# Attention's stores and weight loads on SyncE's queue: when they are issued, and at which heads the side work stands

## The chip, the cores and the metric

The kernel runs on one core of a Trainium2 chip. The metric is the device time of one execution in microseconds (us). The kernel before was run three times: 2304.03, 2305.62 and 2310.8 us, median 2305.62. One further execution was profiled.

The engines go by the profile's names: PE is TensorE's matrix unit, PEld its weight loads, DVE is VectorE, ACT is ScalarE, POOL is GpSimd and SP is SyncE, which here issues every DMA. Each engine runs its own instructions in one fixed order and waits in place for whatever the next one needs. SP does so too, so a DMA whose source is not ready holds up every DMA that stands behind it in SP's order.

## The reference, cut to what matters

```python
h = layernorm(x) * (1 + ca) + sa              # sa, ca, ga, sb, cb, gb = rows of silu(c) @ w_mod
x = x + ga * attention(h)                     # 32 heads of 32, 4 segments of 512 tokens, with a memory
h = layernorm(x) * (1 + cb) + sb
x = x + gb * mixer_mlp(h)                     # an MLP over the 2048 tokens, F = 3584

def attention(h):                             # per head, for s in 0..3:
    p = softmax(q_s @ k_s.T * scale + mask)   # strictly upper triangle masked
    o_s = g * (phi(q_s) @ M / (phi(q_s) @ z + 1e-6)) + (1 - g) * (p @ v_s)
    M, z = M + phi(k_s).T @ v_s, z + sum(phi(k_s))
    return concat(o) @ wo
```

x is 2048 x 1024 in float32. Products are made from operands split into a high and a low part (`split`, L116), three matmuls for one.

## The kernel before, in words

There are three stages: attention, the output projection (`out_proj`, L688), and two large products of the MLP (`mix`, L783). The change touches the first alone.

**How attention is cut.** Four heads of the model make a group `g` (8 groups). A segment of one group is a unit of work `t`; `its` (L313) lists 32 of them: pass 0 takes each group through segments 0 and 1, pass 1 takes each through segments 2 and 3. Head number n = 4t + h runs from 0 to 127. The main loop (L621) goes over n from -3 to 128 and writes down, for each n, the scores of head n, the row maxima of head n + 3, the values of head n - 1 and one of four pieces of projection of the unit that is eight heads ahead.

- `project(t, piece)` (L329): pieces 0 and 1 are the k/v products (`nps`, `kv_chunk` L186, 48 matmuls of 256 columns each; one half takes weight parts v0 for the first 24 and v1 for the others), piece 2 transposes k (`kps`, L363), makes the q product (`qps`, L201, 24 matmuls of 512 columns), splits both into `sg` and calls `stack` for three heads; piece 3 stacks the fourth head and updates the memory. The bank of a k/v product comes free when DVE has subtracted from it (`r`, L356).
- `stack(t, h)` (L319): three DMAs `sk<-sg` (L325 to L327) that lay one head's q and k out for its scores.
- `maxima(t, h)` (L421): products `sx`, `sy`, `sz`, maxima on DVE (L432), and after every second head a transpose `nmps`, two small tiles `nt` (ACT L440, DVE L441) and four DMAs `sk<-nt` (L445), without which the scores of the two heads can't start.
- `scores(t, h)` (L459): products `a` (L466 to L473), exponentials `p` on ACT, the triangle on POOL (L477), a split into `ph` (ACT L479, POOL L481).
- `values(t, h)` (L483): products `pv`; after the fourth head `ot` is copied by ACT (L512) and stored to DRAM (L513).

**Side work at listed heads.** `plan(n, f, engines)` (L594) puts f at head n; `later` (L597) plans a fetch at one head and its use at another. `behind` (L451) lets what f issues on the engines named stand behind the instruction that `marks` keeps for that head: A, G and V stand for ACT, POOL and DVE. The list holds: eight token tiles of the segments of pass 1 (`token_tile`, L227, in the one buffer `gaw`, one tile every 5 heads, stored at once by L246); weights of groups 2 to 7 for pass 0, fetched, split and stored for pass 1 in one go (`keep_w`, L171); 32 tiles of late rows of w_mod (`mod_late`, L523) at heads 40, 42, ... 102; eight pieces of wo (`wo_fetch`, `wo_split`, L575 and L581) at heads 65, 71, ... 107. These share three buffers named `raw`.

**Weights of the second pass.** `load_w` (L176) is called from the loop four heads before a group's first piece stands in it: all six tiles of the group (`wv<-wsp`, `wq<-wsp`, L168) are written down at once. There are eight buffers, so that the last four tiles wait until the group before has been used.

**What sets the order.** The program's order is a priority. A scheduler with a time model walks all engines and gives each the first instruction in that order that its model has ready, so work is pulled ahead where an engine would stand idle. `tc.issue_after(i)` adds the demand that what follows stands behind i on i's engine. What comes out is fixed before the program runs. Where the model's times and the chip's differ, the engine waits.

Of the kernel before, what the change touches and what calls it, by code (L numbers as in the profile page):

```python
# [31 lines left out]
VL = 1  # L32
PHB = 2
P32B = 2
ML0 = 40
MLS = 2
HB = 3
WO0 = 65
WOS = 6
WCT = 5  # L40
LEADP = 8
LEADS = 3
# [2 lines left out]
def attention_and_mlp(ctx, tc, x, wq, wkv, wo, beta, w1, b1, w2, b2, c, wm_a, wm_b, out):  # L45
# [112 lines left out]
            split(w, r[:, 512 * i:512 * i + 512], A, V)  # L158
            W[0, g][kind, 2 * part + i] = w

    def load_part(g, pr, kind, part, res):

        if pr == 0:
            split_part(g, kind, part, fetch_part(g, kind, part))
            return
        for i in range(2):
            w = aw.tile([P, 2, 512], F32R, tag="w", bufs=8, name=f"w{kind}{pr}_{g}_{part}_{i}")
            SY.dma_start(w.bitcast(F32), wsp[g, 2 * part + i if kind == "v" else 4 + i])  # L168
            res[kind, 2 * part + i] = w

    def keep_w(g):  # L171
        for kind, n in (("v", 4), ("q", 2)):
            for i in range(n):
                SY.dma_start(wsp[g, i if kind == "v" else 4 + i], W[0, g][kind, i].bitcast(F32))

    def load_w(g, pr):  # L176
        res = W[pr, g] = {}
        for kind, part in (("v", 0), ("v", 1), ("q", 0)):
            load_part(g, pr, kind, part, res)
        if pr == 0:  # L180
            keep_w(g)

    W = {}

# [42 lines left out]
    def token_tile(tt):  # L227

        r = gaw
        norm_x(a, r)  # L230
        for half in range(2):
            ps = bank("s2", 2, f"hpl{tt}_{half}")
            for i in range(4):
                ct = 4 * half + i
                T.transpose(ps[:, 128 * i:128 * i + 128], r[:, P * ct:P * ct + P], ident)
            for i in range(4):
                ct = 4 * half + i
                A.activation(r[:, P * ct:P * ct + P], ps[:, 128 * i:128 * i + 128], AF.Identity,
                             scale=saca[:, ct, 1:2], bias=saca[:, ct, 0:1])
        hi = a.tile([P, D], F32, tag="raw", bufs=3, name=f"hix{tt}")  # L240
        A.copy(hi.bitcast(F32R), r)
        for c in (slice(0, 512), slice(512, 1024)):
            G.tensor_tensor(r[:, c].bitcast(F32R), r[:, c], hi[:, c], op=ALU.subtract)
        i = tt % 4
        for part, t in enumerate((hi, r)):
# [28 lines left out]
    for ct in range(NK):  # L274
        for part in range(2):
            wm = s1p.tile([P, D], F32, tag="wm", bufs=11, name=f"wm{ct}_{part}")
            last_wm = SY.dma_start(wm, wm_a[part, ct])
            if part == 0:
                V.scalar_tensor_tensor(wm, wm, 1.0, scb, op0=ALU.mult, op1=ALU.mult, accum_out=saca[:, ct, 0:1])
            else:  # L280
                for k in range(NK):
                    T.matmul(scale_ps[:, ct:ct + 1], wm[:, P * k:P * k + P], sc[:, k:k + 1], start=(k == 0),
                             stop=(k == NK - 1), skip_group_check=True)
        if ct < 3:
            load_part(0, 0, *(("v", 0), ("q", 0), ("v", 1))[ct], W[0, 0])
# [29 lines left out]
    st = {}  # L315

    last_sk = {}

    def stack(t, h):  # L319
# [7 lines left out]
        last_sk[t, h] = SY.dma_start(skf[64:96], src[:, 1:3])  # L327

    def project(t, piece):  # L329
        pr, g, seg = its[t]  # L330
# [90 lines left out]
    def maxima(t, h):  # L421
# [20 lines left out]
        for hh in range(2):  # L442
            sk = d["sk", h - 1 + hh]
            for part in range(2):
                SY.dma_start(sk[96 + part:97 + part, 0].bitcast(F32).rearrange("p (b n) -> p b n", n=128),  # L445
                             nt[part][4 * hh:4 * hh + 4].bitcast(F32))

    marks = {}
# [34 lines left out]
    def values(t, h):  # L483
# [26 lines left out]
            T.transpose(ps[:, 128 * i:128 * i + 128], am[:, i], ident)  # L510
        ot = r_.tile([P, L], F32, tag="ot", bufs=1, name=f"ot{t}")
        A.copy(ot, ps)  # L512
        SY.dma_start(oT[g, :, L * seg:L * seg + L], ot)  # L513
        del st[t]

    mcol = const.tile([P, 4 * NK], F32, name="mcol")
# [14 lines left out]
    def mod_rows(lo, hi):  # L531
# [2 lines left out]
        T.transpose(ps[0:n, 0:128], mcol[:, lo:hi], ident)  # L534
        row = pj.tile([n, P], F32, tag="tmp", bufs=2, name=f"mrow{lo}")
        A.copy(row, ps[0:n, 0:128])
        SY.dma_start(modd.rearrange("a (b n) -> (a b) n", n=P)[lo:hi], row)

    def at(f, n):
        if 0 <= n < 4 * NI:  # L540
# [25 lines left out]
    project(1, 2)  # L566
    project(1, 3)
    with tc.issue_after(last_sk[0, 3].ins):
        keep_w(0)
# [11 lines left out]
    def wo_split(i, r):  # L581
# [3 lines left out]
        for j in range(2):  # L585
            G.tensor_tensor(r[:, j], r[:, j], gaw[:, 512 * nh:512 * nh + 512], op=ALU.mult)
            A.copy(hi[:, j].bitcast(F32R), r[:, j])
            V.tensor_tensor(r[:, j].bitcast(F32R), r[:, j], hi[:, j], op=ALU.subtract)
        for part, t in enumerate((hi, r)):
            SY.dma_start(wos[c2:c2 + 2, nh, :, part].rearrange("c p n -> p c n"), t)  # L590

    todo = {}

    def plan(n, f, engines=""):  # L594
        todo.setdefault(n, []).append((f, engines))

    def later(n, fetch, m, f, engines):  # L597

# [2 lines left out]
        plan(m, lambda: f(got[0]), engines)  # L601

    for i in range(8):
        later(5 * i, lambda i=i: SY.dma_start(gaw, x[P * (8 + i):P * (9 + i)]),
              5 * i + 2, lambda r, i=i: token_tile(8 + i), "V")
    for g in range(2, NG):
        n = 8 * g - 13
        plan(n, lambda g=g: W.__setitem__((0, g), {}))
        for kind, part, n0, n1 in (("v", 0, 0, 1), ("v", 1, 1, 3), ("q", 0, 2, 4)):
            later(n + n0, lambda g=g, kind=kind, part=part: fetch_part(g, kind, part),  # L610
                  n + n1, lambda r, g=g, kind=kind, part=part: split_part(g, kind, part, r), "A")
        plan(n + 4, lambda g=g: keep_w(g))
    for j in range(32):
        n = ML0 + MLS * j
        later(n, lambda j=j: mod_fetch(j), n + 2, lambda r, j=j: mod_late(j, r), "V")
    plan(WO0 - 3, lambda: spread(gaw, 0))
    for i in range(8):
        n = WO0 + WOS * i
        later(n, lambda i=i: wo_fetch(i), n + 2, lambda r, i=i: wo_split(i, r), "G")

    for n in range(-LEADS, 4 * NI + VL):  # L621
# [20 lines left out]
        for f, engines in todo.pop(n, ()):  # L642
            with behind(n, engines):
                f()
    right.__exit__(None, None, None)
    for q in skp + [late, prj, paw]:
        q.__exit__(None, None, None)
# [353 lines left out]
```

## Time and profile before

| | us |
|---|---|
| three runs | 2304.03, 2305.62, 2310.8 |
| median | 2305.62 |
| profiled execution | 2305.58 |
| its span, first to last instruction | 2303.9 |
| outside the span | 1.7 |
| PE busy / DVE busy / ACT busy / POOL busy | 2232.7 / 1703.9 / 1105.6 / 727.9 |
| mean granted PE clock | 0.983 |
| attention after the first heads (107 to 1050) | 943 |

Times inside the profile count from the span's first instruction. A row of the timeline gives start, duration, engine, line, operation, tiles (out<-in), form, number of instructions merged and, in brackets, how long the engine had stood idle before it and what ended that. A row of the waits view gives who waited, for whom, the sum, the number of times and the longest. A row of the windows view gives a stretch, its length, the busy time of each engine with its count of instructions, the granted PE clock (1.00 is full speed), the busy share of the DMA engines and their rate. A row of the groups view ends in busy time, mean nanoseconds of one, and idle time before. PE's matmuls overlap each other, so that its busy time is not its work.

### The profile page before, as it was taken

To read this page: it belongs to the slowest core of one execution; us is meant where nothing else is said; L and a number is where in the kernel's file an instruction comes from. 1 tells how busy PE (TensorE), PEld (TensorE's weight loads), DVE (VectorE), ACT (ScalarE), POOL (GpSimd) and SP (SyncE) were. 2 spreads that over 40 slices of the span, in tenths; PEclk is the share of its full clock that TensorE was granted. 3 is DMA by queue.
4 is the path that set the end of the run, shared out by engine and by line. 5 is a ranking of instruction groups with operands and counts; after the bars stand their busy time and mean duration, and the time that the engine had idled before them with its cause. 6 is when DMAs were issued, how large, how long until landed. Compare 5 with 4: busy or idle time off the path is not lost.

```text
span 2303.9 us, 38456 instructions
## 1 busy us (share of the span) xinstructions
PE 2232.7 (97%) x13866; PEld 1918.9 (83%) x13866; DVE 1703.9 (74%) x3814; ACT 1105.6 (48%) x2018; POOL 727.9 (32%) x835
## 2 busy tenths in 40 slices
PE   8989999998999999999999999999999999999999
PEld 7879888898998889977787888888887888888877
DVE  5666666775777777657988665688889787878787
ACT  5477766755656656654324333543334242424232
POOL 3165655655666767653001000023333000000000
PEclk9989999999999999989999999999999999999999
DMA  6656555677566566663466664556557441414133
GB/s 256 199 164 183 173 162 162 195 247 225 156 199 206 166 189 187 202 212 112 137 205 213 249 237 181 202 222 239 206 201 263 171 151 55 151 55 142 55 119 146
DMA packets 172593, 414.67 MB, mean 180 GB/s; under 512 B 17236, under 2 KB 71540, under 8 KB 163444
## 3 DMA queue, kind: packets, MB, share of 16 engines
q1 hardware_dynamic: 172404, 412.22, 54.7%
q8 instruction: 110, 1.80, 0.3%
q14 instruction: 79, 0.65, 0.1%
HBM read 236.23 MB, written 125.06 MB: 157 GB/s over the span
## 4 chain that ended last, share of the span: by engine, by line
PE 81%; DVE 9%; DMA 5%; ACT 2%; issue 1%; POOL 1%; SPq 0%; DVEq 0%; ACTq 0%
PE mx L798 41%; PE nps L193 14%; PE qps L201 7%; PE po L706 6%; PE pv L495 3%; DMA wr<-in_w_dram 1%; PE a L466 1%; PE sx L431 1%; DVE ac L805 1%; PE sz L431 1%; DVE bU L123 1%; PE rd L403 1%; DVE sp L123 1%; DMA sk<-nt 1%; PE a L469 1%
## 5 line engine op out<-in xcount | busy, mean ns | idle before, releaser
L798 PE MATMUL mx<-bU,sp 128*128 128x512 f32 x2352 | 537.0, 390 | 4.7 <-DVE ac L805 2.0
L798 PEld LDWEIGHTS mx<-bU,sp 128*128 128x128 f32 x2352 | 440.4, 188 | 100.8 <-DVE sp L123 2.7
L193 PE MATMUL nps<-wv,h 128*128 128x256 f32 x3072 | 438.2, 284 | 0.7 <-DVE sg L123 0.5
L798 PE MATMUL mx<-bA,sp 128*128 128x512 f32 x1764 | 432.0, 390 | 2.5 <-DVE sp L123 2.2
L120 ACT CAST sp<-wr 128x384 fp32r<-128x384 f32 (+2 forms) x408 | 217.1, 545 | 449.9 <-PE mx L798 379.6
L481 POOL TENSOR_TENSOR ph<-p,ph 128x640 f16<-128x640 f32 x256 | 379.6, 1504 | 159.0 <-ACT ph L479 153.5
L193 PEld LDWEIGHTS nps<-wv,h 128*128 128x128 f32 x3072 | 403.8, 190 | 6.8 <-DVE sg L123 0.7
L798 PEld LDWEIGHTS mx<-bA,sp 128*128 128x128 f32 x1764 | 330.5, 188 | 73.5 <-DVE sp L123 2.9
L123 DVE TENSOR_TENSOR sp<-wr,sp 128x384 fp32r<-128x384 f32 (+2 forms) x408 | 256.8, 641 | 29.4 <-ACT sp L120 29.2
L805 DVE TENSOR_TENSOR ac<-mx,ac 128x512 f32<-128x512 f32 x280 | 189.3, 685 | 91.2 <-PE mx L798 90.5
L201 PE MATMUL qps<-h,wq 128*128 128x512 f32 x768 | 200.7, 406 | 1.4 <-DVE r L356 1.4
L432 DVE CUSTOM_DVE_ANT_0 sx<-sx,mask 128x128 f32<-128x128 f32 (+1 forms) x256 | 109.5, 428 | 113.6 <-PE sx L431 111.9
L706 PE MATMUL po<-wo,ots 128*128 128x512 f32 x768 | 184.8, 400 | 5.3 <-DVE x L709 3.1
L479 ACT CAST ph<-p 128x1280 f16<-128x1280 f32 x128 | 160.8, 1257 | 41.1 <-POOL p L477 40.3
L706 PEld LDWEIGHTS po<-wo,ots 128*128 128x128 f32 x768 | 148.3, 194 | 38.0 <-issue 3.9
L201 PEld LDWEIGHTS qps<-h,wq 128*128 128x128 f32 x768 | 144.4, 194 | 30.2 <-DVE r L356 1.2
L798 PE MATMUL mx<-bB,sp 128*128 128x512 f32 x588 | 164.3, 389 | 0.0
L477 POOL TENSOR_SCALAR_AFFINE_SELECT p<-p 128x256 f32<-128x256 f32 x256 | 120.5, 480 | 129.2 <-ACT p L470 63.4
L495 PE MATMUL pv<-vp,ph 128*128 128x97 bf16 (+1 forms) x2560 | 146.6, 204 | 5.5 <-DVE mv L134 2.7
L495 PEld LDWEIGHTS <-ph 128*128 128x128 f16 x2560 | 117.5, 100 | 29.4 <-issue 12.1
L805 DVE TENSOR_TENSOR cc<-mx,cc 128x512 f32<-128x512 f32 x140 | 94.6, 683 | 49.9 <-PE mx L798 45.4
L798 PEld LDWEIGHTS mx<-bB,sp 128*128 128x128 f32 x588 | 110.4, 188 | 23.4 <-ACT bB L120 0.6
(173 smaller groups left out, 3206.0 us busy)
## 6 DMA issues: line engine op xcount, KB each, us to landing
sk<-sg SPq DMA_DIRECT2D x384, 128.0 KB
wr<-in_w_dram SPq DMA_DIRECT2D x28, 1024.0 KB
wr<-in_w_dram SPq DMA_DIRECT2D x32, 768.0 KB
bstu<-ucd SPq DMA_DIRECT2D x28, 768.0 KB
wsp<-wv SPq DMA_DIRECT2D x32, 512.0 KB
rawm<-in_wm_b_dram SPq DMA_DIRECT2D x32, 512.0 KB
wv<-wsp SPq DMA_DIRECT2D x32, 512.0 KB
pcd<-cc SPq DMA_DIRECT2D x14, 1024.0 KB
```

The lines of the kernel that those rows point to most:

```text
L120: A.copy(hi, src)
L123: lo_eng.tensor_tensor(lo, src, hi.bitcast(F32), op=ALU.subtract)
L193: T.matmul(ps[:, aa], h[:, j, 128 * tt:128 * tt + 128], wt[:, i, o:o + 256], start=(n == 0), stop=(n >= 6 * NK - 2), skip_group_check=True)
L201: T.matmul(ps, wt[:, i, o:o + 128], h[:, j], start=(k + n == 0), stop=(3 * k + n == 3 * NK - 1))
L432: marks[4 * t + h - LEADS, "V"] = V.tensor_tensor_reduce(o, o, mask[:, 384 - 128 * i:], 1.0, -3.0e38, op0=ALU.add, op1=ALU.max, accum_out= ...
L477: G.affine_select(w, w, pattern=[[0, 2], [1, 128]], compare_op=ALU.is_ge, fill=0.0, base=0, channel_multiplier=-1)
L479: marks[n, "A"] = A.copy(ph[:, 0], p32)
L481: marks[n, "G"] = G.tensor_tensor(ph[:, 1, c], p32[:, c], ph[:, 0, c], op=ALU.subtract)
L495: T.matmul(pv[:, i, 0:w], ph[:, part, o:o + 128], d["vp"][:, j, h, 0:w], start=(n == 0), stop=(n == 19), skip_group_check=True)
L706: T.matmul(ps, os_[:, i, P * ct:P * ct + P], wop[ct, nh][:, j], start=(n == 0), stop=(n == 3 * NK - 1))
L798: T.matmul(ps, ops[q][:, i, P * k:P * k + P], b[:, j], start=(m == 0 and first), stop=(m == 3 * nk - 1), skip_group_check=True)
L805: V.tensor_tensor(d, ps, d, op=ALU.add)
```

## The change

- `ot`'s store is planned two heads after the copy, the store of a row tile of the modulation and the stores of `wo` pieces one head after their source, a token tile's store two heads after the tile; all with the engine "S".
- `marks[n, "S"]` is new: the last DMA of `stack` (at the head where it is written down) and the last `sk<-nt` of `maxima`. `behind` takes the nearest mark of the last four heads. So a planned store stands in SP's order behind the sk DMAs of its head.
- `keep_w` becomes `keep_part`, one part at a head: groups 2 to 7 at heads n+5, n+6, n+7 (n = 8g - 13) in place of all at n+4.
- `load_w` and `load_part` go. Group 1 is split at head -3 by `second_group`, without the demand to stand behind the first unit's sk DMAs, and stored at heads 0, 1, 2. The second pass's weights are loaded by `reload_part`: v0 at N, v1 at N+2, q at N+3, N = 8(8+g) - 12, each behind the mark of its head. (N is where `load_w` stood.)
- Token tiles stand at heads 0, 6, ... 42 and use the buffer three heads after the fetch (before: every 5 heads, two heads after).
- The 32 late rows stand at the heads of `MODS`; `wo` pieces at 84, 88, ... 112.
- What is still planned behind the last head is issued after the loop.

```diff
-ML0 = 40
-MLS = 2
+MODS = (23, 25, 31, 37, 40, 42, *range(47, 87, 2), *range(88, 109, 4))
-WO0 = 65
-WOS = 6
+WO0 = 84
+WOS = 4
...
+    def reload_part(g, kind, part):
+
         for i in range(2):
-            w = aw.tile([P, 2, 512], F32R, tag="w", bufs=8, name=f"w{kind}{pr}_{g}_{part}_{i}")
+            w = aw.tile([P, 2, 512], F32R, tag="w", bufs=8, name=f"w{kind}1_{g}_{part}_{i}")
             SY.dma_start(w.bitcast(F32), wsp[g, 2 * part + i if kind == "v" else 4 + i])
...
-        last_sk[t, h] = SY.dma_start(skf[64:96], src[:, 1:3])
+        last_sk[t, h] = marks[4 * t + max(h, 2) - LEADP, "S"] = SY.dma_start(skf[64:96], src[:, 1:3])
...
-                if (n, e) in marks:
-                    s.enter_context(tc.issue_after(marks[n, e].ins))
+                m = next((i for i in range(n, n - 4, -1) if (i, e) in marks), None)
+                if m is not None:
+                    s.enter_context(tc.issue_after(marks[m, e].ins))
...
-        SY.dma_start(oT[g, :, L * seg:L * seg + L], ot)
+        plan(4 * t + 3 + VL + 2, lambda: SY.dma_start(oT[g, :, L * seg:L * seg + L], ot), "S")
...
-        later(5 * i, lambda i=i: SY.dma_start(gaw, x[P * (8 + i):P * (9 + i)]),
-              5 * i + 2, lambda r, i=i: token_tile(8 + i), "V")
+        got = []
+        later(6 * i, lambda i=i: SY.dma_start(gaw, x[P * (8 + i):P * (9 + i)]),
+              6 * i + 3, lambda r, i=i, got=got: got.append(token_tile(8 + i)), "V")
+        plan(6 * i + 5, lambda i=i, got=got: keep_tile(8 + i, got[0]), "S")
...
+            plan(n + 5 + i, lambda g=g, kind=kind, part=part: keep_part(g, kind, part), "S")
+    for g in range(NG):
+        n = 8 * (NG + g) - 12
+        plan(n, lambda g=g: W.__setitem__((1, g), {}))
+        for i, (kind, part) in enumerate(PARTS):
+            plan(n + (0, 2, 3)[i], lambda g=g, kind=kind, part=part: reload_part(g, kind, part), "S")
...
+    plan(-LEADS, second_group)
...
-        if 0 <= m + 4 < 4 * NI:
-            t = (m + 4) // 4
-            if its[t][:2] not in W:
-                with tc.issue_after(last_sk[0, 3].ins):
-                    load_w(its[t][1], its[t][0])
```

More of the change, by code (lines that the diff above doesn't have):

```diff
@@ L159, in split_part, with keep_part @@
             W[0, g][kind, 2 * part + i] = w
[L161 to L165, printed above, removed]
+    def reload_part(g, kind, part):
         for i in range(2):
-            w = aw.tile([P, 2, 512], F32R, tag="w", bufs=8, name=f"w{kind}{pr}_{g}_{part}_{i}")
+            w = aw.tile([P, 2, 512], F32R, tag="w", bufs=8, name=f"w{kind}1_{g}_{part}_{i}")
             SY.dma_start(w.bitcast(F32), wsp[g, 2 * part + i if kind == "v" else 4 + i])
[L169 to L181, printed above, removed]
+            W[1, g][kind, 2 * part + i] = w
+    def keep_part(g, kind, part):
+        for i in (2 * part, 2 * part + 1):
+            SY.dma_start(wsp[g, i if kind == "v" else 4 + i], W[0, g][kind, i].bitcast(F32))
+    PARTS = (("v", 0), ("v", 1), ("q", 0))
     W = {}
@@ L243, in token_tile, with keep_tile @@
             G.tensor_tensor(r[:, c].bitcast(F32R), r[:, c], hi[:, c], op=ALU.subtract)
+        return hi
+    def keep_tile(tt, hi):
         i = tt % 4
-        for part, t in enumerate((hi, r)):
+        for part, t in enumerate((hi, gaw)):
             SY.dma_start(hT1[tt // 4 - 2, :, :, part, P * i:P * i + P].rearrange("k p n -> p k n"),
@@ L568, in attention_and_mlp @@
     with tc.issue_after(last_sk[0, 3].ins):
-        keep_w(0)
+        for kind, part in PARTS:
+            keep_part(0, kind, part)
     right.__exit__(None, None, None)
@@ L619, in attention_and_mlp, with second_group @@
         later(n, lambda i=i: wo_fetch(i), n + 2, lambda r, i=i: wo_split(i, r), "G")
+    def second_group():
+        W[0, 1] = {}
+        for kind, part in PARTS:
+            split_part(1, kind, part, fetch_part(1, kind, part))
+    plan(-LEADS, second_group)
+    for i, (kind, part) in enumerate(PARTS):
+        plan(i, lambda kind=kind, part=part: keep_part(1, kind, part), "S")
     for n in range(-LEADS, 4 * NI + VL):
@@ L644, in attention_and_mlp @@
                 f()
+    for n in sorted(todo):
+        for f, _ in todo[n]:
+            f()
     right.__exit__(None, None, None)
```

28 lines of the change are left out of this document (16 added, 12 removed).

## The prediction

> **What bounds the kernel now.** I read the page first, then windows by stage, then PE's waits and SP's waits inside attention, then the timeline around the worst of them.
>
> ```profile
> span 2303.9 us, 38456 instructions
> ...
> PE 2232.7 (97%) x13866; PEld 1918.9 (83%) x13866; DVE 1703.9 (74%) x3814; ACT 1105.6 (48%) x2018; POOL 727.9 (32%) x835
> ```
>
> PE is busy for 97% of the span, so no change of order can bring more than its idle time, 71 us, and what a lowered clock costs.
>
> ```profile
> 107.00:1050.00 943.00, 906.39 (x7798) 820.52 (x7797) 647.75 (x1964) 609.48 (x1108) 590.59 (x702) 0.97 0.63 186
> ```
>
> This is attention, 128 heads in 943 us, 7.4 us a head. PE (the first busy figure) is idle for 943.00 - 906.39 = 36.6 us, and the granted clock of 0.97 takes some 28 us more. About 65 us, 2.8% of the kernel, is all that this change can touch, since the MLP's order stays. Who ends PE's waits there:
>
> ```profile
> PE a L466 <- DMA sk<-nt: 8.2, 4, 2.8
> PE kps L363 <- DVE r L356: 7.4, 4, 4.1
> PE a L466 <- ACT p L474: 2.6, 2, 1.8
> PE sx L431 <- DMA sk<-sg: 1.5, 1, 1.5
> ```
>
> The scores' wait for the small DMAs `sk<-nt` is the largest: 8.2 us in four waits. SP's own waits in the same stretch show why one suspects the stores:
>
> ```profile
> SPq L513 <- ACT ot L512: 98.5, 21, 12.7
> ...
> SPq L604 <- DMA hT<-gaw: 11.5, 5, 4.5
> ...
> SPq L174 <- DVE wv L123: 10.5, 6, 3.4
> ...
> SPq L537 <- ACT mrow L536: 5.8, 2, 3.4
> ...
> SPq L590 <- ACT woh L587: 5.3, 2, 4.0
> ```
>
> SP stands for 98.5 us before `ot`'s stores and for 21.6 us more before the weights', the rows' and `wo`'s. That is SP's time, not PE's: only where an sk DMA queued behind comes too late does it reach the end.
>
> **Part 1: stores behind the sk DMAs, late rows and wo moved.** These are the places where PE waited for `sk<-nt`, with the DMAs issued just ahead of them:
>
> ```profile
> 523.32 0.56 PE L466 MATMUL a<-sk 98*128 98x512 f32 x1 [1.85 <-DMA sk<-nt]
> 702.54 0.47 PE L466 MATMUL a<-sk 98*128 98x512 f32 x1 [2.21 <-DMA sk<-nt]
> 786.41 0.77 PE L466 MATMUL a<-sk 98*128 98x512 f32 x1 [2.83 <-DMA sk<-nt]
> ```
>
> ```profile
> 516.66 0.39 SPq L520 DMA_DIRECT2D rawm<-in_wm_b_dram  x1
> 517.14 0.38 SPq L168 DMA_DIRECT2D wv<-wsp  x1
> 517.61 2.63 SPq L445 DMA_DIRECT2D sk<-nt  x4
> ```
>
> ```profile
> 780.16 0.45 SPq L578 DMA_DIRECT2D wor<-in_wo_dram  x1
> 780.71 0.41 SPq L520 DMA_DIRECT2D rawm<-in_wm_b_dram  x1
> 781.22 2.63 SPq L445 DMA_DIRECT2D sk<-nt  x4
> ```
>
> Behind large loads the small ones land late. Two of the four waits are followed by a half clock:
>
> ```profile
> 523.60:527.00 3.40, 3.40 (x15) 3.12 (x14) 1.50 (x6) 1.75 (x3) 1.59 (x3) 0.50 0.96 349
> 786.50:789.70 3.20, 3.20 (x26) 2.71 (x27) 0.49 (x2) 2.42 (x4) 0.51 (x1) 0.50 0.00 0
> ```
>
> That is 1.7 and 1.6 us lost, so this class costs 8.2 + 3.3 = 11.5 us at most. At 523 the loads of v1 go away from in front: 1.85 + 1.7 = 3.55 gained. At 702 `wo` moves to head 84 and later, the q load behind the sk DMAs: 2.21 gained. At 786 (about head 90) late row and `wo` piece are now both fetched at head 88, so the pair stays: I take half of 2.83 + 1.6, 2.2. Of the fourth wait (8.2 less the three, 1.3) half, 0.65. Sum **8.6**, bounds 0 and 11.5. The new waits are covered: `ot` has one buffer, its store goes two heads later, and the next copy comes two heads (14.7 us) after that, against 4.7 us that SP waited on average here. A token's `hi` and `wo`'s tiles keep a `raw` buffer one or two heads longer; what stands behind them in SP's order is fetches that are used two heads later. Should a fetch be late for all that, DVE stands before it as in the next part, 2.5 us.
>
> The instructions stay the same in number. Two late rows more than before fall ahead of head 47, each a pass of DVE:
>
> ```profile
> L524 DVE SCALAR_TENSOR_TENSOR rawm<-rawm,scb 128x1024 f32<-128x1024 f32 x32 | 48.2, 1506 | 0.5 <-DMA rawm<-in_wm_b_dram 0.5
> ```
>
> That is 3 us of an engine that is busy for 647.75 of 943; token tiles, thinned from every 5 to every 6 heads, give as much room. I take nothing, bounds 3 either way. At the end `wo`'s last store moves from head 109 to 115; its reload for the output projection stands at head 122, seven heads or 52 us later, so nothing.
>
> **Part 2: token tiles every six heads.** The worst wait of all stands at the second tile:
>
> ```profile
> 143.31 1.11 PE L363 MATMUL kps<-ident,k 128*128 128x128 f32 x4 [4.09 <-DVE r L356]
> 141.77 0.69 DVE L128 BATCH_NORM_STATS2 st<-gaw 128x6 f32<-128x512 f32 x1 [2.51 <-DMA gaw<-in_x_dram]
> ```
>
> DVE stood 2.51 us for the tile's load, with `r` behind it, and PE stood 4.09 us for `r`. After the change the tile is used three heads after its fetch, so that wait goes. Around it the clock was halved:
>
> ```profile
> 125.00:131.00 6.00, 5.70 (x41) 3.80 (x40) 5.46 (x23) 5.81 (x14) 4.95 (x4) 1.00 0.48 161
> 131.10:148.00 16.90, 11.08 (x46) 8.14 (x46) 10.77 (x30) 11.38 (x19) 12.38 (x16) 0.50 0.66 188
> ```
>
> 8.45 us is lost to it. It began before the wait, so I take a quarter of it: 4.1 + 2.1 = **6.2** gained, bounds 0 and 14.1 (all of it, with the 1.5 for `sk<-sg`). The fetch now waits for a store planned one head before it; its use is 22 us later, against a longest wait of 4.5 (L604 above). Group 1's earlier fetch I take at nothing, bound 0.8, which is what ACT waited for it:
>
> ```profile
> 82.84 1.14 ACT L120 CAST wv<-rawv 128x512 fp32r<-128x512 f32 x2 [0.78 <-DMA rawv<-in_wkv_dram]
> ```
>
>
> **Part 3: the second pass's v1 behind the stack.** This costs. The products of unit t begin when the q product of t - 1 ends, and reach v1 24 matmuls later. Now v1 is issued behind the third head's stack of t - 1:
>
> ```profile
> 715.76 0.59 SPq L327 DMA_DIRECT2D sk<-sg  x1
> ```
>
> ```profile
> 419.31 4.39 DMA rawm<-in_wm_b_dram
> ```
>
> With that load's 4.39 us (half a MB, as v1's tiles), v1 is there at 716.35 + 4.4 = 720.8. Before, the first matmul on it started at 713.0. Over all eight groups of the pass, from the first matmul on v1 to that landing, `nps` alone:
>
> ```profile
> 530.70:553.60 22.90, 10.06 (x74) 8.90 (x72) 1.00 0.81 250
> ...
> 713.00:720.80 7.80, 6.44 (x40) 5.54 (x41) 1.00 0.86 184
> ...
> sum 93.30, PE 62.11 PEld 55.14; mean PE 7.76 PEld 6.89
> ```
>
> The eight counts add to 431 matmuls that would have to be done later, of this length:
>
> ```profile
> 68.77 5.01 PE nps L193 x44
> ```
>
> 431 x 0.114 = 49 us of projection is pushed back. The other half's first 24 need only v0 and can come forward: 8 x 24 x 0.114 = 22 us. What is left, 27 us, must be filled by heads pulled forward. How well do heads alone fill PE? Three stretches of the second pass between `nps` and `qps` show it:
>
> ```profile
> 697.40:703.20 5.80, 3.59 (x38) 2.76 (x37) 5.80 (x17) 2.92 (x8) 4.21 (x4) 1.00 0.92 345
> 783.20:790.30 7.10, 4.27 (x35) 3.52 (x33) 2.35 (x9) 3.95 (x8) 2.14 (x5) 0.76 0.33 130
> 842.90:849.40 6.50, 4.58 (x55) 3.57 (x51) 5.91 (x18) 5.45 (x11) 4.80 (x7) 1.00 0.01 1
> ```
>
> PE is idle for 6.96 of 19.4 us, or 1.9 without the two `sk<-nt` waits, which are counted above: 10 to 36%. That gives 2.7 to 9.8 us; I take 4, since the order is made with the late load in the model, and 2 for the clock (one fall like that at 786). **6** lost. Bounds: 0, and all 49 us at 36% idle and a tenth for the clock, 22. The group at 530 is the worst, its sk DMAs being late in any case.
>
> On the clock the Trainium skill says otherwise: "TensorE: Matmul & The Clock Gate", section "Why this matters for your kernels", wants PE-idle gaps of over about 3 us for a fall of the clock. By that rule part 3 would lose no clock and the sum would be 2 us lower. This trace speaks against it: at 131.1 the clock fell with PE busy for 5.70 of the 6.00 us before.
>
> **Sum.** -8.6 - 6.2 + 6 = -8.8 us. The profiled execution took 2305.58 (span 2303.9 and 1.7 around it), the same as the median of 2305.62: 2305.6 - 8.8 = **2297**.
>
> **The rivals.**
>
> Slower: v1 late is dearer than I take it. Nothing but projections fills PE between heads; if the other half's first 24 don't come forward and each group's stretch runs like the three above, 49 us at 36% and the clock, 22, and the savings come to half, 7.4, because rows and pieces meet at head 88 and after: 2305.6 + 22 - 7.4 = 2320. It decides from the point where part 3 costs more than the 14.8 of parts 1 and 2. For it: in every group the q product of t - 1 ends before its stack begins, so v1 is never early. Against it: the program puts a stack six heads, 44 us, ahead of its first scores, so there are heads to pull forward.
>
> Faster still: a steadier SP queue closes other stretches without projections. The nine longest that I found in both passes:
>
> ```profile
> sum 77.60, PE 55.74 PEld 43.12 DVE 64.16 ACT 59.82 POOL 54.10; mean PE 6.19 PEld 4.79 DVE 7.13 ACT 6.65 POOL 6.01
> ```
>
> 21.9 us of PE idle; 6.1 of it stands from 125 to 145 (part 2) and 5.0 are `sk<-nt` (part 1). If the rest, 10.8, went too: 2297 - 11 = 2286. For it: the DMAs bunch. Against it: most waits there are for DVE and ACT, which keep their work.
>
> No change: SP's waits lie off the path. 98.5 us of waiting for `ot` has PE waiting only 8.2 us, and the loads that stand ahead of `sk<-nt` are as large as before. Then a few us saved go into part 3: 2305. The same comes out if the scheduler had put most stores behind the sk DMAs anyway.
>
> **How the numbers follow.** Forecast (2289 to 2302) 0.36, slower (2310 to 2330) 0.28, faster still (2275 to 2289) 0.22, no change 0.14. A measurement of this kernel tells about 0.3%, 7 us, from no change: that line lies at 2298.7, inside the forecast, which gives 0.28 of its 0.36 to faster. Faster 0.28 + 0.22 = 0.50; same 0.08 + 0.14 = 0.22; slower 0.28. The range for 8 in 10 goes from all of parts 1 and 2 with half of part 3's 6 (2305.6 - 25.6 + 3 = 2283), with two thirds of the faster rival's 11 below that, 2276, up to the slower rival's 2320.
>
> **What would show it.** Right: SP's wait for `ot` near nothing, `sk<-nt` waits of PE under 3 us, no half clock of 17 us near head 6. Part 3 shows in PE's waits as `nps <- DMA wv<-wsp`, or as stretches with heads alone before the 25th matmul of units 16, 18, ... 30. Wrong: idle of PE in attention above 36.6 us, or more half clocks in the second pass than before.

## The result and the profile after

The changed kernel takes 2333.6 us (median of four runs, 2329.97 to 2342.19) against 2306.7 of the kernel before (four runs). The ratio is 1.0123, with a 95% interval of 1.0104 to 1.0141: 27 us slower, where 9 us faster were forecast. The profiled execution took 2333.03 us.

The head of the page after:

```profile
span 2331.3 us, 38429 instructions
...
PE 2239.5 (96%) x13866; PEld 1920.1 (82%) x13866; DVE 1703.6 (73%) x3814; ACT 1106.8 (47%) x2018; POOL 725.6 (31%) x835
```

The work is the same, the span 27.4 us longer. The windows view of the changed kernel, attention from 107 us to its last head (1076 here, 1050 before):

```profile
107.00:1076.00 969.00, 913.88 (x7802) 820.95 (x7801) 646.07 (x1969) 609.28 (x1106) 586.88 (x700) 0.97 0.62 184
```

Attention is 26 us longer. PE's idle time there grew from 36.6 to 969.00 - 913.88 = 55.1 us, and the granted clock stayed at 0.97, so the loss isn't clock: 18.5 us of it are idle time, and 7.5 stand in PE's busy time at the same number of matmuls. PE's waits in that stretch, after:

```profile
PE nps L183 <- DMA wv<-wsp: 13.3, 8, 3.0
PE sy L426 <- DVE mx L427: 8.9, 11, 3.6
PE a L461 <- DMA sk<-nt: 7.8, 5, 3.6
PE pv L490 <- DVE red L497: 4.1, 5, 1.5
PE sx L426 <- DVE mx L427: 3.6, 9, 0.9
PE kps L358 <- DVE r L351: 2.4, 3, 1.1
```

Four things are to be seen. The first row is new: k/v products wait for the second pass's tiles. By the places of the waits in PE's order of products, 7.5 us of it are for v1 and 5.8 for v0. The wait for `sk<-nt`, which part 1 was to close, is 7.8 us where it was 8.2. The wait for `r` fell from 7.4 to 2.4. And the waits for DVE's row maxima (`mx`) come to 12.5 us in two rows. Before, there were such rows too, between those that the prediction shows, 9.6 us together:

```profile
PE sz L431 <- DVE mx L432: 4.7, 5, 2.3
PE sx L431 <- DVE mx L432: 2.8, 6, 0.6
...
PE sy L431 <- DVE mx L432: 2.1, 5, 1.1
```

So `sk<-nt` was the longest single row before, but the three rows for `mx` together were longer, and nothing in the change was aimed at them. SP's longest wait, after:

```profile
SPq L440 <- ACT nt L435: 98.5, 21, 8.9
```

The 98.5 us in front of `ot`'s stores are gone from the list. SP now stands in front of the DMAs `sk<-nt` themselves, until ACT has made `nt`, by chance for as long. What SP stands for has changed, and PE's wait for `sk<-nt` is nearly the same. The windows view of the changed kernel around the second token tile, where the clock had been halved for 17 us:

```profile
125.00:131.00 6.00, 4.54 (x49) 3.51 (x48) 5.38 (x21) 6.00 (x15) 4.21 (x6) 1.00 0.51 153
131.10:148.00 16.90, 16.44 (x132) 13.64 (x131) 13.53 (x34) 15.19 (x26) 14.33 (x17) 1.00 0.76 218
```

That place is cured, as part 2 said. What DVE waits for token tiles from 107 to 560 us, before and then after:

```profile
DVE st L128 <- DMA gaw<-in_x_dram: 2.5, 1, 2.5
```

```profile
DVE st L127 <- DMA gaw<-in_x_dram: 6.4, 3, 2.9
```

The wait that was to go has grown. A tile's store is now held behind the sk DMAs, and the next tile's load into the same buffer stands behind it in SP's order. In one of the three waits, at 401 us, SP stood for the landing of that store before it issued the load. In the two others the store had been issued 16 and 17 us ahead of the load. There the load came late by what else stood ahead of it in SP's order. SP ahead of the longest of the three, which ends at 259.94 us:

```profile
239.04 1.40 SPq L239 DMA_DIRECT2D hT<-gaw  x1
240.50 2.71 SPq L169 DMA_DIRECT2D wsp<-wv  x2
...
249.41 2.64 SPq L440 DMA_DIRECT2D sk<-nt  x4
...
254.79 0.59 SPq L605 DMA_DIRECT2D gaw<-in_x_dram  x1
```

From the tile's store to the next tile's load SP issues one DMA after the other (the rows left out are `sk<-sg`). SP also has a new wait of its own in front of weight fetches, until the tile's part `hix`, which takes one of the three `raw` buffers, is stored; before, this was 0.5 us:

```profile
SPq L150 <- DMA hT<-hix: 10.8, 3, 4.3
```

### The profile page after: what moved, and what is told of

Same layout as the page of the kernel before. It is cut to its first block, busy times and chain, and to the rows that moved or that the text cites. A ratio compares the mean times of both kernels' runs of the same rounds, so it can differ in the third digit from the quotient of the medians.

```text
span 2331.3 us, 38429 instructions
## 1 busy us (share of the span) xinstructions
PE 2239.5 (96%) x13866; PEld 1920.1 (82%) x13866; DVE 1703.6 (73%) x3814; ACT 1106.8 (47%) x2018; POOL 725.6 (31%) x835
## 4 chain that ended last, share of the span: by engine, by line
PE 79%; DVE 8%; DMA 6%; ACT 2%; issue 2%; SPq 1%; POOL 1%; DVEq 0%; ACTq 0%; POOLq 0%
PE mx L812 43%; PE nps L183 12%; PE qps L191 7%; PE po L720 5%; PE pv L490 3%; DMA wv<-wsp 1%; PE sx L426 1%; PE a L461 1%; PE sz L426 1%; DVE bU L122 1%; DMA sk<-nt 1%; PE rd L398 1%; DMA x<-in_x_dram 1%; PE a L464 1%; PE sy L426 1%
## 5 line engine op out<-in xcount | busy, mean ns | idle before, releaser
L812 PEld LDWEIGHTS mx<-bU,sp 128*128 128x128 f32 x2352 | 440.7, 188 | 97.6 <-DVE sp L122 2.2
L183 PE MATMUL nps<-wv,h 128*128 128x256 f32 x3072 | 437.9, 285 | 15.5 <-DMA wv<-wsp 13.3
L427 DVE CUSTOM_DVE_ANT_0 sx<-sx,mask 128x128 f32<-128x128 f32 (+1 forms) x256 | 110.5, 431 | 87.9 <-PE sx L426 84.9
L462 ACT ACTIVATE p<-a,shift 128x512 f32<-128x512 f32 x128 | 88.1, 688 | 99.8 <-PE a L461 53.5
```

Source lines behind the costliest of these rows:

```text
L183: T.matmul(ps[:, aa], h[:, j, 128 * tt:128 * tt + 128], wt[:, i, o:o + 256], start=(n == 0), stop=(n >= 6 * NK - 2), skip_group_check=True)
L427: marks[4 * t + h - LEADS, "V"] = V.tensor_tensor_reduce(o, o, mask[:, 384 - 128 * i:], 1.0, -3.0e38, op0=ALU.add, op1=ALU.max, accum_out= ...
L812: T.matmul(ps, ops[q][:, i, P * k:P * k + P], b[:, j], start=(m == 0 and first), stop=(m == 3 * nk - 1), skip_group_check=True)
```

## The experiments

To say where a kernel lost time, PE's rows give marks that every variant has: the first `nps` of units 2, 13, 16 and 18, the last `nps` of unit 30, the last head's first score, and the end of the output projection (us between them, from the traces; the time is the median). After each expectation below stand the median, its ratio to the kernel before, and the 95% interval of that ratio. Each group of experiments had its own runs of the kernel before beside it, with medians of 2304.7 to 2306.7.

| kernel | time | 2 to 13 | 13 to 16 | 16 to 18 | 18 to 30 | 30 to last head | to end of projection |
|---|---|---|---|---|---|---|---|
| before | 2306 | 355.6 | 86.1 | 67.2 | 368.0 | 88.8 | 171.2 |
| after | 2333.6 | 350.8 | 97.6 | 71.3 | 373.9 | 98.2 | 174.8 |
| e1 reload undone | 2328.2 | 351.4 | 101.9 | 62.6 | 367.3 | 104.3 | 170.1 |
| e2 tiles undone | 2334.3 | 360.3 | 87.9 | 72.3 | 372.3 | 102.6 | 172.9 |
| e3 rows, wo undone | 2326.3 | 351.1 | 100.1 | 62.5 | 379.4 | 94.7 | 168.5 |
| e4 before + reload | 2332.3 | 358.5 | 84.5 | 65.2 | 381.4 | 93.5 | 177.9 |
| e5 before + stores | 2331.8 | 371.5 | 87.9 | 68.6 | 367.7 | 93.1 | 175.2 |
| e6 before + tiles | 2301.5 | 342.4 | 91.7 | 65.6 | 367.4 | 91.9 | 171.8 |
| e7 before + rows, wo | 2320.6 | 356.6 | 87.2 | 60.0 | 371.5 | 106.5 | 170.4 |
| e8 before, rows shifted | 2318.9 | 359.1 | 85.3 | 69.1 | 371.2 | 93.1 | 173.9 |
| e9 stores but tiles' | 2314.5 | 356.4 | 86.8 | 72.4 | 365.2 | 91.9 | 173.4 |
| e10 before, wo shifted | 2309.1 | 357.8 | 85.1 | 66.9 | 363.8 | 96.3 | 173.0 |
| e11 e6, rows shifted | 2304.8 | 344.0 | 95.7 | 63.3 | 364.7 | 94.6 | 174.9 |
| e12 after, v1 early | 2318.8 | 348.6 | 98.4 | 69.9 | 361.6 | 97.4 | 172.9 |
| e13 after, tiles at once | 2326.6 | 343.9 | 102.6 | 63.8 | 372.9 | 101.4 | 173.5 |
| e14 e12 and e13 | 2316.6 | 344.7 | 102.9 | 61.0 | 360.3 | 105.8 | 173.8 |
| e15 e14 and e3 | 2319.9 | 343.9 | 101.0 | 61.5 | 376.4 | 97.0 | 174.2 |
| e16 after, rows shifted | 2326.2 | 348.6 | 98.5 | 66.0 | 375.0 | 96.5 | 172.3 |
| e17 e4, v1 early | 2305.0 | 358.1 | 83.6 | 61.2 | 366.5 | 94.9 | 171.6 |
| e18 e16, v1 early | 2308.4 | 348.3 | 99.2 | 63.6 | 357.7 | 100.2 | 171.2 |

Two limits of the table: each row is one execution, which lay within 3.5 us of its median, and the marks are those of the projections, so that work of the heads can move across them. At the first `nps` of unit 16, PE had begun 218 score products `a` before, 213 after and 224 in e13. With some 0.6 us of PE for a head's four scores and 0.7 for its twenty values (start to start, in the traces), I estimate that up to 4 us of a difference can be moved work.

By the table the change won 4.8 us in the first pass and lost 11.5 at the turn of the passes (units 13 to 16, about heads 42 to 54), 4.1 and 5.9 in the second pass, 9.4 among the last heads, 3.6 behind them. Theory A at the start: the late reload of v1 carries the loss. Its rivals: B, the places of the side work; and, formed after the first runs, F, that the order before fits its waits closely, so that any edit that shifts it loses; and G, that the held-back stores of the token tiles cost.

**Undoing one part of the change.** e1, the reload:

```diff
-            plan(n + (0, 2, 3)[i], lambda ...: reload_part(g, kind, part), "S")
+            plan(n, lambda ...: reload_part(g, kind, part))
```

> The changed kernel with part 3 alone undone: all six weight tiles of a second-pass group are again written down together, four heads ahead of the group's first projections, and no longer behind the stack's DMAs. Theory A (the late reload leaves PE without projections; it shows as 13.3 us of PE waiting in nps for wv, and as a lag that grows in the second pass): 2333.6 falls by 14 to 24, to 2310 to 2320, and the wait of nps for wv goes to nothing. Theory B (the cost comes from where token tiles, late rows and pieces of wo now stand; the reload only moves waits about): 2333 within 5, with other waits in the place of nps <- wv.

2328.2, ratio to before 1.0098 (1.0073 to 1.0123). The wait for `wv` is gone and the stretch from 16 to 30 is 15.3 us shorter, but the turn and the last heads give back 4.3 and 6.1 of it. The time is at the edge of B's range (2328 to 2338) and outside A's, while the place of the gain is A's. e2, the token tiles (5i, 5i + 2, stored at once):

> The changed kernel with the token tiles as before: one every five heads, used two heads after its fetch and stored at once, so that the last one stands at head 35 and no longer at head 42, where it meets the last weights of the first pass. Theory B (placement): the 12 us that were lost from 440 to 560 go, and the 17 us half clock near head 6 may come back for 4 to 8: 2333.6 falls by 4 to 12, to 2322 to 2330. Theory A (late reload): within 3 of 2333.6, or up to 8 slower when the half clock near head 6 comes back.

2334.3, 1.013 (1.0105 to 1.0154): no gain, as A said, and outside B's range. The turn of the passes is 9.7 us shorter and the first pass 9.5 longer, 2 to 3 us of each being moved work by the estimate above. So the time at the turn is where the tiles' gain of the first pass is given back. e3, rows and pieces (`MODS = range(40, 104, 2)`, `WO0, WOS = 65, 6`):

> The changed kernel with the late rows at every second head from 40 on and the pieces of wo at every sixth from 65 on, as before. Theory B (placement): the 5.5 us that the last 80 us of attention lost go, and a few us where rows and weights met at heads 40 to 50: 2324 to 2330. Theory A (late reload): within 4 of 2333.6.

2326.3, 1.0086 (1.0065 to 1.0108), 7 gained, as B said for its size; but e16 below gains as much by an edit that means nothing.

**One part alone in the kernel before.** e4, the reload (the marks, and `load_part` planned at n, n + 2, n + 3 behind them):

> The kernel before with part 3 alone: the second pass's tiles in three portions behind the stack's and the maxima's DMAs (v0 at the same head as before, v1 two heads later, q three heads later); stores, token tiles, rows and wo stay. Theory A (late reload): 2306.7 rises by 14 to 24, to 2321 to 2331, and nps waits for wv by some 10 us or more. Theory B (placement): within 5 of 2306.7. What the prediction took for this part was 6, 2313.

2332.3, 1.0109 (1.0087 to 1.0131): 1 us above theory A's range, with 8.1 us of waiting for `wv`, and more than four times the 6 that the prediction took. e5, all stores, with tiles every five heads; e6, the tiles; e7, rows and pieces; e8, a neutral edit (`ML0 = 41`):

> The kernel before with part 1's stores alone: every store of attention (ot, weights, token tiles, rows, wo) is queued one or two heads behind its source and behind the small sk DMAs; reload, token tiles, late rows and wo stand where they stood before (group 1's early fetch is in it). What the prediction took for it is the place at 523 and half of the one at 786 or so: 2306 falls by 3 to 8. Theory A (the late reload carries the loss, the rest is near nothing): 2298 to 2308. Theory F (the order before fits its waits closely, and any edit that shifts the order of the engines loses 10 to 25 in waits and half clocks at other places): 2315 to 2330.

> The kernel before with part 2 alone: token tiles every six heads, used three heads after their fetch. The prediction took 6 gained (the 17 us half clock near head 6). Theory A: 2298 to 2306. Theory F (any shift of the order loses 10 to 25): the half clock near head 6 goes and the time is still 2310 to 2325, with new waits at heads 40 to 50 and in the last 100 us of attention.

> The kernel before with the late rows and the pieces of wo at the listed heads alone (wo from head 84 every four, rows from 23 to 108). The prediction took nothing, 3 either way. Theory A: 2303 to 2310. Theory F: 2315 to 2330. Undoing this part in the changed kernel gained 7, so theory B (placement) says 2310 to 2316.

> A neutral edit: the kernel before with its late rows at heads 41, 43, ... 103 in place of 40, 42, ... 102, the same work one head later. Theories A and B: within 4 of 2306. Theory F (the order before fits closely and any shift loses): 2312 or more, up to 2330, with half clocks at other places than before.

e5 2331.8, 1.0115 (1.0094 to 1.0137); e6 2301.5, 0.9978 (0.9964 to 0.9993); e7 2320.6, 1.0056 (1.0039 to 1.0074), with 17.7 lost among the last heads alone; e8 2318.9, 1.0047 (1.0030 to 1.0064). e7 and e8 fall into F's ranges, e5 2 us above its own; e6 falls into A's and against F. Part 2 alone gains about what was forecast for it; it beats both kernels. The stores, forecast to gain, cost as much as the reload. e8 moves one set of passes by one head and costs 12. The four parts alone come to 26 + 26 - 5 + 14 = 61 us, together they cost 27: they don't add. In e5 the loss stands in the first pass (15.9 of it). DVE's wait for tiles from 107 to 560 us, e5:

```profile
DVE st L127 <- DMA gaw<-in_x_dram: 12.4, 5, 3.4
```

In e6, whose tiles are stored at once, DVE has no such wait. So e9: e5 with the tiles' stores at once; and e10, a second neutral edit (`WO0 = 66`); e11, e6 with e8's shift; e12, the changed kernel with v1's two heads given back:

```diff
-            plan(n + (0, 2, 3)[i], lambda ...: reload_part(g, kind, part), "S")
+            plan(n + (0, 0, 3)[i], lambda ...: reload_part(g, kind, part), "S")
```

> The kernel before with the stores of ot, weights, rows and wo behind the small sk DMAs, but the token tiles' stores at once as before (the run that queued all stores had, with tiles every five heads, only one head between a tile's store and the next tile's load, and DVE waited 6.8 us for that load). Theory G (the stores of the tiles were what cost there): 2306 to 2316. Theory F (any shift of the order loses 10 to 25, the place doesn't matter): 2315 to 2332.

> A second neutral edit: the kernel before with its pieces of wo at heads 66, 72, ... 108 in place of 65, 71, ... 107. It leaves everything ahead of head 60 as it is. Theory F (the order before fits closely): 2311 to 2322, the loss from head 66 on and most of it in the last 100 us of attention. Against it: within 4 of 2306.

> Token tiles every six heads alone (2301.5 by itself) and the late rows one head later (2318.9 by itself). If part 2's gain is a thing of its own (the wait for the second tile and its half clock, some 6 to 8 us by the stretch to head 9), it stays beside the neutral edit: 2318.9 less 5, 2312 to 2316. If it was only another lucky or unlucky order, theory F: anywhere from 2305 to 2325, with no relation to the stretch near head 6.

> The changed kernel with v1's second-pass reload planned at the head of v0's, two heads earlier, still behind the small DMAs of that head; v0 and q as changed. If part 3's cost is v1's lateness (theory A): nps waits for wv fall from 13.3 to under 3, and the stretch from 600 to 960 gains the 7 us that undoing the whole reload gained there; 2333.6 goes to 2322 to 2328. If it is the portions as such, or v0 behind the DMAs: within 4 of 2333.6, with nps still waiting.

e9 2314.5, 1.0039 (1.0025 to 1.0052): G's range, 17 less than e5, 15.1 of it in the first pass, and DVE's wait for tiles falls to 2.0 us. The other stores still cost 8, which is less than what the neutral edit e8 moved. e10 2309.1, 1.0016 (1.0007 to 1.0026): below F's range; the last stretch lost 7.5, units 18 to 30 gained 4.2. e11 2304.8, 0.9991 (0.9978 to 1.0005), 14 below e8 and below both ranges: part 2's gain in the first pass (355.6 or 359.1 to 344.0) stands in another order too, and the rest isn't explained. e12 2318.8, 1.0052 (1.0039 to 1.0066): 15 less than the changed kernel, 12.3 of it in units 18 to 30, by an edit of one digit. That is more than theory A's range asked for. `nps` still waits once for `wv`, 3.7 us, at the first product of the second pass (unit 16).

**What adds.** e13, the changed kernel with tiles stored at once (`keep_tile` called where `token_tile` is); e14, that and v1 early; e15, that and e3; e16, a neutral edit of the changed kernel (`MODS` one higher each):

> The changed kernel with the token tiles stored at once, three heads after their fetch, in place of two heads later behind the small DMAs; all else as changed. Theory G (the postponed store holds the next tile's load, DVE waits 6.4 us for that load in three waits, and the order of heads 10 to 50 pays for it): DVE's waits for the load go, 2333.6 falls by 6 to 17, to 2317 to 2328, the gain ahead of 540 us. Theory A alone (v1's lateness carries the loss): within 5 of 2333.6.

> Both at once: v1's reload at the head of v0's (2318.8 by itself) and the token tiles stored at once. If the two costs stand side by side, A and G: 2302 to 2313. If they are one cost, or only the order's luck (F): 2315 to 2325.

> The run before it with late rows and pieces of wo back at their old heads as well (worth 7 in the changed kernel, 13 in the kernel before). If the three costs add: 2295 to 2306, which would beat the kernel before; what is left of the change then is the stores of ot, weights, rows and wo behind the small DMAs, and the token tiles every six heads. Theory F: 2308 to 2325.

> A neutral edit of the changed kernel: its late rows one head later each. It says how far an order without any meaning moves this time. In the kernel before, two such edits cost 11 and 3. Theory F: 2322 to 2345. If the changed kernel's time is set by the named waits: 2330 to 2338.

e13 2326.6, 1.0101 (1.0082 to 1.0119); e14 2316.6, 1.0057 (1.0038 to 1.0076); e15 2319.9, 1.0068 (1.0049 to 1.0087); e16 2326.2, 1.0094 (1.0076 to 1.0112). The five kernels with tiles every six heads stored at once (e6, e11, e13 to e15) have a first pass of 342.4 to 344.7; the six of that period with held-back stores have 348.3 to 351.4. In the two pairs that differ by this alone the held-back store costs 6.9 us (after and e13) and 3.9 (e12 and e14) there; e13 gives 5.0 back at the turn, most of it moved work, and DVE still waits 3.8 us for tiles in it. e14 gains 2 on e12, e15 nothing more: A and G together and the sum of three costs both said less time than came out, and F's ranges held. The parts' prices don't add. e16 gains 7.5 and means nothing (F's range again), so the 5 to 7 of e1, e3 and e13 can't be told from the order's chance. Of the edits of the changed kernel only v1's is larger. So it was tried in two other orders, e17 (e4 with the digit) and e18 (e16 with it):

> The reload by portions alone in the kernel before (2332 by itself), but v1 at the head of v0. In the changed kernel v1's two heads were worth 15. If v1's lateness is a cost of its own (theory A), it shows in this order too: 2332 less 10 to 20, 2312 to 2322, and the stretch from 600 to 960 falls from 44.8 us of loss to under 36. If the 15 were the order's chance (theory F): 2322 to 2335.

> The changed kernel with the late rows one head later (2326 by itself) and v1 at the head of v0. Theory A: 2326 less 10 to 20, 2306 to 2316. Theory F: 2318 to 2335.

e17 2305.0, 0.9998 (0.9985 to 1.0010), 27 less than e4; e18 2308.4, 1.0016 (1.0004 to 1.0028), 18 less than e16. With e12 (15) and e14 against e13 (10), the digit gains in four orders out of four. In units 18 to 30 the gains are 14.9 (e4 to e17), 12.3 (after to e12), 17.3 (e16 to e18) and 12.6 (e13 to e14). Theory A holds: v1's two heads of delay are a cost of their own. A fifth pair is weaker: from e3 to e15, where the tiles' stores differ too, the time falls by 6 and units 18 to 30 by 3.0 alone. The 8.1 us of waiting for `wv` go there, but PE's wait for `sk<-nt` in these units grows from 2.8 to 9.0. And e18 bears on the rest of the change: with stores, tiles and places as changed, but the rows one head on and v1 early, the kernel takes 4 us more than the kernel before. The windows view for units 18 to 30, e4 and then e17:

```profile
592.30:973.70 381.40, 368.06 (x3230) 336.53 (x3229) 258.47 (x807) 229.37 (x408) 250.09 (x302) 0.98 0.62 178
```

```profile
586.70:953.20 366.50, 360.41 (x3238) 331.95 (x3237) 264.07 (x808) 228.22 (x405) 249.90 (x301) 1.00 0.63 184
```

The same for the changed kernel and e12:

```profile
603.70:977.60 373.90, 360.37 (x3209) 329.06 (x3208) 252.84 (x799) 225.78 (x404) 244.92 (x295) 1.00 0.60 172
```

```profile
601.30:962.90 361.60, 357.62 (x3218) 330.62 (x3218) 255.15 (x804) 228.50 (x407) 245.49 (x300) 1.00 0.60 176
```

PE is idle for 13.3 and 13.5 us with v1 late, 6.1 and 4.0 with v1 early (8.2 before). In the changed kernel 7.6 of the 13.5 are waits for `wv`, 4.7 for v1 and 2.8 for v0. The rest of the difference is PE's busy time, 7.7 and 2.8 us longer where v1 is late. In e4 this is nearly all clock: 17 us at half clock in these units against 3.4 in e17, so 8.5 us lost against 1.7. In the changed kernel and e12 the clock is full in these units, and the 2.8 us aren't explained.

**What the late tiles do to the order.** PE's order of the k/v products in a group's first unit (matmuls, group 2 in the second pass; e12 has before's order):

```
before: half 0: v0 24, v1 24; half 1: v0 24, v1 24
after:  half 0: v0 24; half 1: v0 24; half 0: v1 12; half 1: v1 9; half 0: v1 12; half 1: v1 15
```

The other half's first 24 do come forward, 23 or 24 of them, in every group. But then both halves end together. ACT's copies of the two halves of that unit, in the timeline before:

```profile
656.75 0.36 ACT L349 COPY k<-nps 128x256 f32<-128x256 f32 x1
657.00 0.39 ACT L350 COPY v<-nps 128x256 f32<-128x256 f32 x1
667.57 0.36 ACT L349 COPY k<-nps 128x256 f32<-128x256 f32 x1
```

and after:

```profile
680.01 0.37 ACT L344 COPY k<-nps 128x256 f32<-128x256 f32 x1 [1.47 <-PE nps L183]
680.28 0.38 ACT L345 COPY v<-nps 128x256 f32<-128x256 f32 x1
682.21 0.37 ACT L344 COPY k<-nps 128x256 f32<-128x256 f32 x1 [0.79 <-PE nps L183]
```

Half 0 is copied 2.2 us ahead of half 1, where it was 10.8. All that follows from it bunches behind the unit's last matmul, beside the heads' own work. The order and the copies are shown; that this bunching makes what the waits for the tile itself leave of the 15 us is argued from them, not tried by itself.

## Why the prediction was wrong, point by point

**Part 1 failed, and by the subtraction below it is the larger miss.** Its step "at 523 the loads of v1 go away from in front ... 3.55 gained" and the two like it priced four waits for `sk<-nt` as if taking the stores and loads away from in front of them would end them. PE still waits 7.8 us for `sk<-nt`, at other places. The longest in the timeline after, with the last part of `nt` that it needs and what SP issued between:

```profile
196.62 0.77 PE L461 MATMUL a<-sk 98*128 98x512 f32 x1 [3.60 <-DMA sk<-nt]
```

```profile
182.28 0.28 DVE L436 SCALAR_TENSOR_TENSOR nt<-nmps,nt 8x128 fp32r<-8x128 f32 x1 [2.07 <-ACT nt L435]
```

```profile
184.75 1.07 SPq L169 DMA_DIRECT2D wsp<-wq  x2
185.86 0.95 SPq L508 DMA_DIRECT2D oT<-ot  x1
186.91 1.11 SPq L320 DMA_DIRECT2D sk<-sg  x1
188.06 1.25 SPq L321 DMA_DIRECT2D sk<-sg  x1
189.35 1.19 SPq L322 DMA_DIRECT2D sk<-sg  x1
190.59 0.57 SPq L239 DMA_DIRECT2D hT<-hix  x1
191.27 0.60 SPq L239 DMA_DIRECT2D hT<-gaw  x1
191.98 3.83 SPq L440 DMA_DIRECT2D sk<-nt  x4
```

`nt` was ready at 182.56 us, and its DMAs were issued from 191.98 on. All that time SP was issuing other DMAs, without a pause. A store that is held behind one head's sk DMAs stands ahead of the next head's, and the prediction had no term for the time that SP's issues take. Stores stand so in this one place of five. In three of the others only `sk<-sg` stand right ahead of `sk<-nt`, and in the fifth (1011 us) SP issued them as soon as `nt` was ready.

All stores but the tiles' behind the sk DMAs (e9) cost 8 us rather than gain 8.6; the 8 is within what a neutral edit moves, the 16.6 between the two figures is more. And "the new waits are covered" failed for the token tiles: I gave a late fetch 2.5 us of DVE, with no price for PE, and took it that only fetches with time to spare stand behind the store in SP's order; DVE waits 6.4 us in the changed kernel and 12.4 in e5, and the first pass pays 4 to 7 us in the one (e12 against e14, after against e13) and 15 in the other (e5 against e9). Rows and pieces, taken at "nothing, bounds 3 either way", cost 14 alone (e7). In the changed kernel, 27 less v1's 15 and with part 2's 5 added back leaves 17 for stores and places together, where -8.6 stood; as the parts don't add, this is a rough figure. How the 17 divides stays open: undoing either moves the time by no more than a neutral edit does, and e18 shows that with v1 early a neutral edit takes most of it away.

**Part 2 was right in its place; its number came out partly by luck.** Forecast 6.2, e6 measured 5. In the first pass it is 13.2 (355.6 to 342.4), twice the forecast, some 3 us of it moved work by the estimate above; 5.6 is given back at the turn and 3 at the last heads, for which the forecast had no term. Of the 17 us half clock, of which I took a quarter (2.1), 6.8 us are left in e6, 5.1 gained where 2.1 was taken, and none in the changed kernel. The windows view of e6, in what is left:

```profile
133.70:140.40 6.70, 6.42 (x24) 5.10 (x25) 4.42 (x16) 4.94 (x11) 5.21 (x9) 0.50 0.78 246
```

**Part 3 had the right mechanism and half the size or less.** Forecast 6, measured 15 in the changed kernel, 10, 18 and 27 in other orders. Of its terms, the 4 for idle time measured 9.5 in the changed kernel's units 18 to 30 (after against e12) and 7.2 in e4 (against e17); the 2 for the clock measured nothing in the one and 6.8 in the other. The step "27 us must be filled by heads ... 10 to 36%, I take 4, since the order is made with the late load in the model" failed: the 22 us came forward as supposed, but the 27 us were priced at the idle share of stretches in which a unit's two halves still ended 11 us apart. And the order, though made with the late load in its model, still put products where PE waits for their tiles, 7.6 us in these units. The bound of 22 would have covered the changed kernel, and not e4.

The longest wait for v1 in the changed kernel's units 18 to 30, in the timeline:

```profile
852.77 0.96 PE L183 MATMUL nps<-wv,h 128*128 128x256 f32 x6 [1.77 <-DMA wv<-wsp]
```

On the clock, the Trainium skill ("TensorE: Matmul & The Clock Gate", section "Why this matters for your kernels") warns of a fall of the clock after PE gaps of over about 3 us, by which part 3 would lose no clock. In the changed kernel's units 18 to 30 it lost none: the granted clock is 1.00 in its row for these units, with gaps of at most 1.82 us in front of the late tiles (the longest is for v0, in unit 30). So far the trace agrees. In e4 it did lose some, in four falls. One of them stands at a gap of 3.0 us, the others at smaller ones. The windows view of e4, ahead of one fall and in it:

```profile
726.30:736.30 10.00, 8.25 (x72) 7.02 (x70) 7.29 (x24) 7.19 (x16) 8.09 (x9) 1.00 0.91 327
736.40:739.70 3.30, 3.30 (x8) 2.58 (x9) 1.97 (x5) 2.72 (x4) 1.96 (x5) 0.50 0.90 294
```

PE's idle time in the 10 us ahead of that fall is 1.75 us in all, so there the measurement differs from the page's figure.

**The rivals.** "Slower" came out in its direction, past its 2320 and its 2330. v1 late was dearer, but not for the reason it gave: the other half's first 24 did come forward. Its savings at half were too kind. Its condition was well put: part 3 cost more than parts 1 and 2 saved. "Faster still" fell, since PE's idle time in attention grew from 36.6 to 55.1 us. "No change" failed in its number, but was right about `ot`: the 98.5 us that SP stood for it are gone, and PE's wait for `sk<-nt` went from 8.2 to 7.8 only.

**What should have been a term.** The order before is worth something by itself. Three neutral edits moved the time by +12, +3 and -7.5 us. The last heads, 88.8 us before, are 91.9 to 106.5 in the nineteen other kernels. A change that moves 32 row passes, 8 pieces and all stores draws such an order anew, and the prediction gave that nothing. Why the last heads are shortest in the order before isn't settled.

## What to carry to other kernels

In a kernel whose PE is 97% busy under a fixed order, ask of a load not only when its first reader needs it but how late readers regroup: here two heads of delay made both halves of a product end together and cost 10 to 27 us, by one digit. A store that is held back is also the release of its buffer, and it stands in its queue ahead of what comes next; follow both, to the next load into that buffer and to the next small DMA behind it, before calling it free. And measure a neutral shift or two first: what such an edit moves (here up to 12 us) is the least that a forecast's range must hold, and the least that an experiment must move to mean something.

## What the runs showed of the hardware that was not expected

A half clock can follow hard on one long gap, or stand where there is none. In the changed kernel the longest of the falls among the last heads stands at a gap of 3.56 us (timeline, then the window after it):

```profile
1046.22 0.58 PE L426 MATMUL sy<-sk 96*128 96x256 f32 x1 [3.56 <-DVE mx L427]
```

```profile
1045.90:1062.90 17.00, 15.34 (x73) 11.84 (x74) 13.67 (x44) 8.16 (x15) 9.25 (x11) 0.50 0.52 191
```

and the one at 736.4 in e4 (quoted above) stands after 1.75 us of idle time in 10 us, all gaps together, none above 0.8. Beyond that the hardware did nothing new: the surprise was the order's.
